# Merged products, another formula for |w|, an early one-column sine and a later modulation step in the generation of an S4 convolution kernel

## The chip, the core and the metric

The program runs on one core of one Trainium2 chip. Its metric is the device time of one execution in microseconds (us). A core has five engines with their own instruction streams: TensorE (PE in the profile, with weight loads as PEld), VectorE (DVE), ScalarE (ACT), GpSimd (POOL) and SyncE (SP). Here SyncE and GpSimd mainly issue DMAs. TensorE's clock is granted by a throttle; the profile gives it as a share of full speed.

## The reference

A block with 512 channels over 2048 positions: a layer norm with modulation, a long convolution per channel whose kernel K is built from a diagonal state space model, then a mixer and an MLP. The change lies in how K is built.

```python
dt = exp(log_dt)[:, None]
A, Bc, Cc = A_re + 1j*A_im, B_re + 1j*B_im, C_re + 1j*C_im
logdA, dB = dt * A, dt * Bc
P = exp(logdA[:, :, None] * l[None, None, :])        # l = 0 .. 2047
K = einsum("dn,dnl,dn->dl", Cc, P, dB).real          # 512 channels, 128 states
...
mod = (silu(c) @ w_mod).reshape(1, 6, 1, 512)
h = layernorm(x) * (1 + ca) + sa
x = x + ga * ssm_conv(h)                              # y = conv(h, K) + h * Dskip
...
```

With w = Cc * B, a channel's K[l] is the real part of a sum over 128 states of dt * w * exp(dt * A * l). Position l is split into a fine part (64 values) and a coarse one (32 values); the sum over states is then a matmul between a coarse factor, which carries w, and a fine one.

## The kernel before

The program has a preparation (lines 282 to 412), the generation loop (lines 531 to 564), and the transforms, the convolution, the mixer and the MLP behind it. All of it stands in an order written out by hand: each engine runs its instructions in the order of the program, and an instruction waits for the tiles that it needs.

*Preparation.* VectorE works on tiles of 128 x 512 (four groups of 128 channels on the partitions, 128 states each). It forms dt*A, w (`wr`, `wi`), the absolute values `ax`, `ay`, their larger `mc` and smaller `mn`, the ratio (with a first reciprocal, line 368), its arctangent `at0` on ScalarE, and out of it the phase of w in turns (`at`, lines 386 to 394). The weight |w| dt is `wn`: ScalarE takes the cosine of `at0`, VectorE its reciprocal (line 400), times `mc`, times dt. TensorE transposes `wn` (line 406) and ScalarE evicts it to `WN`. The phases are split into a high and a low part (`hilo`) and placed by matmuls with permutations (line 358, tiles `px`), evicted to `T1S`. In between, the modulation vectors are formed (`mod_parts`, `mod_sum`); lines 411 and 412 multiply two of them by a third.

*The loop.* A chunk k is 16 channels, 32 chunks in all; four chunks make a group t of 64 channels. For each chunk:

- `turns(k, cos)` forms the phase of both factors in turns with matmuls (lines 462 and 463, two halves of the array at a time; constants added and subtracted round them to the nearest turn), and ScalarE takes the sine or the cosine of the two 512 columns at once. It runs two chunks ahead.
- `exps(t, ...)` forms the magnitudes for a whole group on TensorE and ScalarE (five pieces), once in four chunks, in the chunk with k % 4 == 1. Sine and exponential need different tables of ScalarE, so the table is loaded twice per group (ACT_TABLE_LOAD).
- `weigh(t)` multiplies a part of the magnitudes by `WN` (line 261).
- `products(k)` on VectorE: `m1`, the coarse magnitude, as an outer product of two small factors (line 478); the fine factor `e0` with the sine in both signs (two instructions on line 482) and with the cosine (line 484); the coarse factor `e1` with the sine (483) and the cosine (485).
- `burst(k, ...)`: 64 small matmuls sum over the states (line 502); every second chunk ScalarE evicts the result to `KX`.
- `fill(n)`: n matmuls into a tile that is overwritten later (line 491), which keep TensorE busy.
- `side[k]`: the normalization of the input u (lines 423 to 430), its first transform (`u_dft`, evicted to `vs`, written to DRAM), and loads. `later` and `now` put evictions one chunk later.

Work tiles are rotated: `xx` (PSUM) has two buffers, the sine's and the cosine's tiles three, `e0` and `e1` two, `m1` one.

Of the kernel before, what the change touches and what calls it, by code (L numbers as in the profile page):

```python
# [109 lines left out]
def body(ctx, tc, A):  # L110
# [171 lines left out]
    with tc.manual_schedule():  # L282
# [59 lines left out]
        wr, wi, t0, t1 = tmp("wr"), tmp("wi"), tmp("t0"), tmp("t1")  # L342
        V.tensor_mul(wr, cr, br)
# [42 lines left out]
        V.tensor_scalar(at, at0, INV2PI, None, op0=OP.mult)  # L386
# [13 lines left out]
        V.reciprocal(wn, wn)  # L400
        V.tensor_mul(wn, wn, mc)
# [9 lines left out]
        V.tensor_mul(mods[1], mods[1], mods[2])  # L411
        V.tensor_mul(mods[0], mods[0], mods[2])
# [40 lines left out]
    def turns(k, cos):  # L453
        t, u = divmod(k, 4)
        r0 = slice(u // 2 * 64, u // 2 * 64 + 64)
        r1 = slice(64 - r0.start, 128 - r0.start)
        l0, l1, c = T0S[r0, t], T1S[r1, t * 2 + k % 2], slice(k % 2 * 512, k % 2 * 512 + 512)
        x = psx.tile([128, 1024], F32, name="xx")
        ops = [(l0, C0[r0, c], l1, C1[r1])] + [(ON[r0, i], MG[r0], ON[r1, i], MG[r1]) for i in (2, 0, 1)[1 - cos:]]
        ops.append((l0, C0N[r0, c], l1, C1N[r1]))  # L460
        for i, (la, ma, lb, mb) in enumerate(ops):
            T.matmul(x[:, :512], la, ma, start=(i == 0), stop=(i == len(ops) - 1))  # L462
            T.matmul(x[:, 512:], lb, mb, start=(i == 0), stop=(i == len(ops) - 1))  # L463
# [4 lines left out]
    trig = {}  # L468

    def products(k):  # L470
# [5 lines left out]
        f2 = lambda z: z.rearrange("p a b -> p (a b)")  # L476
        m1 = wk1.tile([128, 16, 32], F32, name="m1")
        V.tensor_mul(m1.rearrange("p d (x y) -> p d x y", x=4),
                     pt[:, :, None, :8].to_broadcast([128, 16, 4, 8]),
                     pt[:, :, 8:12, None].to_broadcast([128, 16, 4, 8]))  # L480
        for a in range(2):
            V.scalar_tensor_tensor(e0[:, 1, a], sn[:, 0], 1.0 - 2.0 * a, mg[:, a], op0=OP.mult, op1=OP.mult)  # L482
        V.tensor_mul(f2(e1[:, 1]), sn[:, 1], f2(m1))
        V.tensor_mul(e0[:, 0], cs[:, 0:1].to_broadcast([128, 2, 512]), mg)  # L484
        V.tensor_mul(f2(e1[:, 0]), cs[:, 1], f2(m1))  # L485
# [45 lines left out]
    with tc.manual_schedule():  # L531
        for k in range(2):
            trig[k] = turns(k, 0), turns(k, 1)
        weigh(0)
        for k in range(33):
            now, later = later, []
            if 1 in KP:
                fill(3)
            for f in now:
                f()  # L540
            if k + 2 < 32:
                trig[k + 2] = turns(k + 2, 0), turns(k + 2, 1)
            if k < 32:
# [622 lines left out]
```

## Time and profile before

| | |
|---|---|
| median of 3 runs | 769.93 us (769.35 to 771.09) |
| the profiled execution | 766.72 us, of it 764.9 us of span |
| mean granted TensorE clock | 0.952 |
| TensorE busy | 693.8 us (91%) |
| VectorE busy | 512.9 us (67%) |
| ScalarE busy | 332.8 us (44%) |
| GpSimd busy | 98.1 us (13%) |

The span is the time from the first to the last instruction. The shares are means over stages with different limits: in the preparation and the loop, the first 222 us, VectorE is nearly always busy, behind it TensorE alone. A row of the timeline reads: start, duration (both in us), engine, line, operation, written tile <- read tiles, sizes, count; in brackets the time the engine sat idle before it and what it waited for. A row that groups instructions ends with the busy time, the mean duration in ns and the idle time before. ACTIVATE instructions all carry line 118, that of a helper, and are told apart by their tiles: `sn` and `cs` are sine and cosine, `p` the magnitudes.

### The profile page before, as it was taken

To read this page: it belongs to the slowest core of one execution; us is meant where nothing else is said; L and a number is where in the kernel's file an instruction comes from. 1 tells how busy PE (TensorE), PEld (TensorE's weight loads), DVE (VectorE), ACT (ScalarE), POOL (GpSimd) and SP (SyncE) were. 2 spreads that over 40 slices of the span, in tenths; PEclk is the share of its full clock that TensorE was granted. 3 is DMA by queue.
4 is the path that set the end of the run, shared out by engine and by line. 5 is a ranking of instruction groups with operands and counts; after the bars stand their busy time and mean duration, and the time that the engine had idled before them with its cause. 6 is when DMAs were issued, how large, how long until landed. Compare 5 with 4: busy or idle time off the path is not lost. (4 is left out here: it accounts for less than half of the span.)

```text
span 764.9 us, 17371 instructions
## 1 busy us (share of the span) xinstructions
PE 693.8 (91%) x7340; PEld 540.2 (71%) x7340; DVE 512.9 (67%) x883; ACT 332.8 (44%) x540; POOL 98.1 (13%) x194
## 2 busy tenths in 40 slices
PE   2799999999989999995578799999999999999993
PEld 1356666665569656662368698999999998998992
DVE  8999999999873576774695696655565545353611
ACT  3678888887843445533133453312223121212120
POOL 1011121110000001000145110112021010100101
PEclk9999999999995899998789799999999999999997
DMA  9523282645259994884316701111110111101001
GB/s 299 164 66 83 71 235 77 168 131 149 57 130 258 243 334 152 274 251 167 137 40 230 246 29 28 29 38 46 32 52 15 42 29 28 28 28 28 9 20 27
DMA packets 51301, 85.51 MB, mean 112 GB/s; under 512 B 5300, under 2 KB 37944, under 8 KB 49560
## 3 DMA queue, kind: packets, MB, share of 16 engines
q1 hardware_dynamic: 44808, 57.92, 27.3%
q0 software_dynamic: 6416, 26.48, 10.5%
q8 instruction: 58, 0.95, 0.5%
q14 instruction: 19, 0.16, 0.1%
HBM read 58.17 MB, written 31.85 MB: 118 GB/s over the span
## 5 line engine op out<-in xcount | busy, mean ns | idle before, releaser
L118 ACT ACTIVATE gh<-pm 128x512 fp32r<-128x512 f32 (+1 forms) x48 | 26.9, 561 | 202.1 <-PE pm L784 202.1
L781 PE MATMUL pm<-nh,w3h 128*128 128x256 f32 (+1 forms) x352 | 87.9, 283 | 0.4 <-ACT nh L118 0.4
L782 PE MATMUL pm<-nh,w3l 128*128 128x256 f32 (+1 forms) x352 | 87.4, 281 | 0.0
L885 DVE TENSOR_TENSOR gl<-gf,gh 128x512 fp32r<-128x512 f32 (+1 forms) x48 | 30.9, 643 | 72.0 <-ACT gf L118 72.0
L894 PE MATMUL pa<-w4h,gh 128*128 128x512 f32 (+1 forms) x176 | 69.5, 395 | 0.0
L895 PE MATMUL pa<-w4l,gh 128*128 128x512 f32 (+1 forms) x176 | 68.9, 391 | 0.0
L781 PEld LDWEIGHTS pm<-nh,w3h 128*128 128x128 f32 (+1 forms) x352 | 65.4, 186 | 2.0 <-ACT nh L118 0.6
L782 PEld LDWEIGHTS pm<-nh,w3l 128*128 128x128 f32 (+1 forms) x352 | 65.6, 186 | 1.7
L784 PE MATMUL pm<-nl,w3h 128*128 128x256 f32 (+1 forms) x352 | 56.1, 282 | 0.0
L784 PEld LDWEIGHTS pm<-nl,w3h 128*128 128x128 f32 (+1 forms) x352 | 47.8, 186 | 0.1
L900 PE MATMUL pa<-w4h,gl 128*128 128x512 f32 (+1 forms) x176 | 47.8, 390 | 0.0
L462 PE MATMUL xx<-MG,ON 64*128 64x512 f32 x160 | 47.4, 391 | 0.0
L463 PE MATMUL xx<-MG,ON 64*128 64x512 f32 x160 | 47.4, 391 | 0.0
L482 DVE SCALAR_TENSOR_TENSOR e<-sn,p 128x512 f32<-128x512 f32 x64 | 41.2, 685 | 4.7 <-ACT sn L118 4.7
L841 DVE TENSOR_TENSOR h<-h,ph 128x512 f32<-128x512 f32 x16 | 11.0, 688 | 45.9 <-PE ph L840 45.9
L502 PEld LDWEIGHTS kp<-e,e 128*32 128x32 f32 x2048 | 30.1, 110 | 14.7 <-issue 9.7
L118 ACT ACTIVATE p<-xx 128x1024 f32<-128x1024 f32 (+1 forms) x40 | 38.2, 983 | 4.3 <-PE xx L254 3.1
L648 DVE TENSOR_TENSOR ma<-pk,us 128x512 f32<-128x512 f32 x32 | 21.9, 686 | 26.0 <-issue 18.2
L484 DVE TENSOR_TENSOR e<-cs,p 128x1024 f32<-128x1024 f32 x32 | 39.0, 1218 | 0.0
L118 ACT ACTIVATE z<-pz 128x512 f32<-128x512 f32 x32 | 17.4, 595 | 49.6 <-issue 33.9
L502 PE MATMUL kp<-e,e 128*32 128x64 f32 x2048 | 35.5, 221 | 2.8 <-DVE e L485 1.9
L900 PEld LDWEIGHTS pa<-w4h,gl 128*128 128x128 f32 (+1 forms) x176 | 33.0, 188 | 6.9
(223 smaller groups left out, 1862.5 us busy)
## 6 DMA issues: line engine op xcount, KB each, us to landing
VU<-vs SPq DMA_DIRECT2D x64, 128.0 KB, 2.6
ld<-VU SPq DMA_DIRECT2D x32, 256.0 KB, 8.2
ZT<-z POOLq DMA_DIRECT2D x16, 512.0 KB, 4.6
ld<-ZT SPq DMA_DIRECT2D x16, 512.0 KB, 5.6
Dw<-in_w POOLq DMA_DIRECT2D x8, 688.0 KB, 4.6
xu<-in_u SPq DMA_DIRECT2D x16, 256.0 KB, 6.7
KX<-in_u SPq DMA_DIRECT2D x16, 256.0 KB, 10.1
GD<-go POOLq DMA_DIRECT2D x16, 256.0 KB, 2.7
```

Source lines behind the costliest of these rows:

```text
L118: return S.activation(out, in_, f, bias=bias, scale=scale)
L462: T.matmul(x[:, :512], la, ma, start=(i == 0), stop=(i == len(ops) - 1))
L463: T.matmul(x[:, 512:], lb, mb, start=(i == 0), stop=(i == len(ops) - 1))
L482: V.scalar_tensor_tensor(e0[:, 1, a], sn[:, 0], 1.0 - 2.0 * a, mg[:, a], op0=OP.mult, op1=OP.mult)
L484: V.tensor_mul(e0[:, 0], cs[:, 0:1].to_broadcast([128, 2, 512]), mg)
L502: T.matmul(kp[32 * j:32 * j + 32, (k % 2) * 4 + g], e1[:, r, d], e0[:, r, :, d * 32:d * 32 + 32], start=(r == 0), stop=(r == 1), skip_grou ...
L781: T.matmul(p, wh[:, k, c], hi[k], start=(k == 0), stop=False)
L782: T.matmul(p, wl[:, k, c], hi[k], start=False, stop=False)
L784: T.matmul(p, wh[:, k, c], lo[k], start=False, stop=(k == 3))
L894: T.matmul(acc[i], gh[:m, e, s], W4h[:m, f], start=(f == 0), stop=False)
L895: T.matmul(acc[i], gh[:m, e, s], W4l[:m, f], start=False, stop=False)
L900: T.matmul(acc[i], gl[:m, e, s], W4h[:m, f], start=False, stop=(f == 10))
```

## The change

In the preparation, |w| becomes mc * cos(at0) + mn * sin(at0), with a second sine on ScalarE (`ws`) in the place of the reciprocal; the ratio goes to `mx` so that `mn` lives on; the scaling of the arctangent to turns moves from VectorE to ScalarE; `wn` and `ws` lie in columns of KX. The transposes of the weights and the third modulation vector move behind the first turns, and the two multiplications of modulation vectors to the end of chunk 1. In the loop, sine and cosine share one tile, so that the coarse factor is one product of 1024 columns; `m1` is formed for two chunks at once; the two sine products of the fine factor come first, and the first weighing behind them. A sine of a single column (`turn1`) follows the five magnitudes of a group. Of twelve fillers a group, five are left.

```diff
@@ preparation
+        wn, ws = KX[:, 7168:7680], KX[:, 7680:]
...
-        V.tensor_mul(mn, mn, mx)
-        at, at0, wn = tmp("at"), tmp("at0"), tmp("wn")
-        act(at0, mn, AF.Arctan)
+        V.tensor_mul(mx, mn, mx)
+        at, at0 = tmp("at"), tmp("at0")
+        act(at0, mx, AF.Arctan)
+        act(at, at0, scale=INV2PI)
         act(wn, at0, AF.Sin, scale=-1.0, bias=hpi)
+        act(ws, at0, AF.Sin)
...
-        V.tensor_scalar(at, at0, INV2PI, None, op0=OP.mult)
...
-        V.reciprocal(wn, wn)
         V.tensor_mul(wn, wn, mc)
+        V.tensor_mul(ws, ws, mn)
+        V.tensor_add(wn, wn, ws)
         V.tensor_tensor(as4(wn), as4(wn), by(dt), op=OP.mult)
-        wps = psu.tile([128, 512], F32, name="pu")
-        for i in range(4):
-            s = slice(i * 128, (i + 1) * 128)
-            T.transpose(wps[:, s], wn[:, s], ident)
-        act(WN, wps)
-        mod_parts(2)()
-        mod_sum(2)()
-        load_u(1)
-        V.tensor_mul(mods[1], mods[1], mods[2])
-        V.tensor_mul(mods[0], mods[0], mods[2])
@@ turns
-        o = wk.tile([128, 2, 512], F32, name="cs" if cos else "sn", bufs=3)
-        act(o.rearrange("p a b -> p (a b)"), x, AF.Sin, scale=-TWO_PI, bias=hpi if cos else 0.0)
-        return o
+        if not cos:
+            trig[k] = wk.tile([128, 2, 2, 512], F32, name="tr", bufs=3)
+        act(trig[k][:, 1 - cos].rearrange("p a b -> p (a b)"), x, AF.Sin, scale=-TWO_PI, bias=hpi if cos else 0.0)
...
+    turn1 = wk1.tile([128, 1], F32, name="turn1")
@@ products
-        sn, cs = trig.pop(k)
-        mg, pt = PE[t][0][u], PE[t][1][:, u]
+        tr = trig.pop(k)
+        mg = PE[t][0][u]
...
-        m1 = wk1.tile([128, 16, 32], F32, name="m1")
-        V.tensor_mul(m1.rearrange("p d (x y) -> p d x y", x=4),
-                     pt[:, :, None, :8].to_broadcast([128, 16, 4, 8]),
-                     pt[:, :, 8:12, None].to_broadcast([128, 16, 4, 8]))
         for a in range(2):
-            V.scalar_tensor_tensor(e0[:, 1, a], sn[:, 0], 1.0 - 2.0 * a, mg[:, a], op0=OP.mult, op1=OP.mult)
-        V.tensor_mul(f2(e1[:, 1]), sn[:, 1], f2(m1))
-        V.tensor_mul(e0[:, 0], cs[:, 0:1].to_broadcast([128, 2, 512]), mg)
-        V.tensor_mul(f2(e1[:, 0]), cs[:, 1], f2(m1))
+            V.scalar_tensor_tensor(e0[:, 1, a], tr[:, 1, 0], 1.0 - 2.0 * a, mg[:, a], op0=OP.mult, op1=OP.mult)
+        if k == 0:
+            weigh(0)
+        if u % 2 == 0:
+            m1 = m1s[0] = wk1.tile([128, 2, 512], F32, name="m1")
+            pt = PE[t][1][:, u:u + 2].rearrange("p a d c -> p (a d) c")
+            V.tensor_mul(m1.rearrange("p a (d x y) -> p (a d) x y", x=4, y=8),
+                         pt[:, :, None, :8].to_broadcast([128, 32, 4, 8]),
+                         pt[:, :, 8:12, None].to_broadcast([128, 32, 4, 8]))
+        V.tensor_mul(e0[:, 0], tr[:, 0, 0:1].to_broadcast([128, 2, 512]), mg)
+        V.tensor_mul(e1.rearrange("p r d q -> p r (d q)"), tr[:, :, 1], m1s[0][:, u % 2:u % 2 + 1].to_broadcast([128, 2, 512]))
         return e0, e1
@@ the loop
-        for k in range(2):
-            trig[k] = turns(k, 0), turns(k, 1)
-        weigh(0)
+        turns(0, 0)
+        turns(0, 1)
+        wps = psu.tile([128, 512], F32, name="pu")
+        for i in range(4):
+            T.transpose(wps[:, i * 128:i * 128 + 128], wn[:, i * 128:i * 128 + 128], ident)
+        act(WN, wps)
+        late = mod_parts(2)
+        turns(1, 0)
+        late()
+        late = mod_sum(2)
+        turns(1, 1)
+        late()
+        load_u(1)
         for k in range(33):
             now, later = later, []
-            if 1 in KP:
-                fill(3)
...
             if k + 2 < 32:
-                trig[k + 2] = turns(k + 2, 0), turns(k + 2, 1)
+                turns(k + 2, 0)
+                turns(k + 2, 1)
...
                     fill(3)
                     for u in range(2, 5):
                         exps(k // 4 + 1, u, u + 1)
-                        fill(2)
+                        if u < 4:
+                            fill(1)
+                    act(turn1, hpi, AF.Sin)
...
+            if k == 1:
+                V.tensor_mul(mods[1], mods[1], mods[2])
+                V.tensor_mul(mods[0], mods[0], mods[2])
             for f in side[k]:
                 f()
```

More of the change, by code (lines that the diff above doesn't have):

```diff
@@ L463, in turns @@
             T.matmul(x[:, 512:], lb, mb, start=(i == 0), stop=(i == len(ops) - 1))
-        o = wk.tile([128, 2, 512], F32, name="cs" if cos else "sn", bufs=3)
-        act(o.rearrange("p a b -> p (a b)"), x, AF.Sin, scale=-TWO_PI, bias=hpi if cos else 0.0)
-        return o
+        if not cos:
+            trig[k] = wk.tile([128, 2, 2, 512], F32, name="tr", bufs=3)
+        act(trig[k][:, 1 - cos].rearrange("p a b -> p (a b)"), x, AF.Sin, scale=-TWO_PI, bias=hpi if cos else 0.0)
     trig = {}
+    turn1 = wk1.tile([128, 1], F32, name="turn1")
+    m1s = {}
     def products(k):
         t, u = divmod(k, 4)
-        sn, cs = trig.pop(k)
-        mg, pt = PE[t][0][u], PE[t][1][:, u]
+        tr = trig.pop(k)
+        mg = PE[t][0][u]
         e0 = wk.tile([128, 2, 2, 512], F32, name="e0")
         e1 = wk.tile([128, 2, 16, 32], F32, name="e1")
-        f2 = lambda z: z.rearrange("p a b -> p (a b)")
-        m1 = wk1.tile([128, 16, 32], F32, name="m1")
-        V.tensor_mul(m1.rearrange("p d (x y) -> p d x y", x=4),
-                     pt[:, :, None, :8].to_broadcast([128, 16, 4, 8]),
-                     pt[:, :, 8:12, None].to_broadcast([128, 16, 4, 8]))
-        for a in range(2):
[L482 to L485, printed above, removed]
+        for a in range(2):
+            V.scalar_tensor_tensor(e0[:, 1, a], tr[:, 1, 0], 1.0 - 2.0 * a, mg[:, a], op0=OP.mult, op1=OP.mult)
[9 more added lines that the diff above has]
+        V.tensor_mul(e1.rearrange("p r d q -> p r (d q)"), tr[:, :, 1], m1s[0][:, u % 2:u % 2 + 1].to_broadcast([128, 2, 512]))
         return e0, e1
```

## The prediction

> **What bounds the kernel now.** I read the page first, then the busy times by stretch, one stretch for each of the eight groups of 64 channels of the generation loop (cut where the weighing on line 261 runs, so a stretch holds four chunks), then VectorE's instructions in order of time, then ScalarE's and TensorE's around a change of group.
>
> ```profile
> 86.60:108.30 21.70, 20.93 (x313) 13.27 (x317) 21.37 (x35) 17.97 (x21) 3.38 (x5) 1.00 0.64 180
> ...
> 177.60:200.90 23.30, 21.85 (x368) 13.82 (x371) 21.62 (x34) 18.78 (x22) 3.04 (x5) 1.00 0.52 145
> 200.90:222.50 21.60, 19.75 (x429) 12.54 (x421) 18.78 (x27) 15.55 (x21) 0.00 (x0) 1.00 0.27 57
> sum 180.50, PE 173.36 PEld 108.80 DVE 172.04 ACT 147.50 POOL 26.02; mean PE 21.67 PEld 13.60 DVE 21.50 ACT 18.44 POOL 3.25
> ```
>
> A row has the stretch and its length, then the busy time (and count) of TensorE, its weight loads, VectorE, ScalarE and GpSimd, and TensorE's granted clock. The loop is 180.5 of the 764.9 us of the span. VectorE is busy 172.0 of it and TensorE 173.4, so two engines share the bound, with ScalarE at 147.5 behind. But part of TensorE's time is filler: 84 matmuls of line 491 whose result nobody reads. In a group where VectorE has enough other work the stretch is VectorE's sum (21.37 of 21.70); later groups last 23.3 for much the same 21.6.
>
> One chunk of VectorE's work in the steady state, and the first and the last of eight places where two chunks follow each other directly:
>
> ```profile
> 87.76 0.66 DVE L478 TENSOR_TENSOR m<-p 128x512 f32<-128x512 f32 x1
> 88.33 1.29 DVE L482 SCALAR_TENSOR_TENSOR e<-sn,p 128x512 f32<-128x512 f32 x2
> 89.54 0.69 DVE L483 TENSOR_TENSOR e<-sn,m 128x512 f32<-128x512 f32 x1
> 90.14 1.22 DVE L484 TENSOR_TENSOR e<-cs,p 128x1024 f32<-128x1024 f32 x1
> 91.28 0.69 DVE L485 TENSOR_TENSOR e<-cs,m 128x512 f32<-128x512 f32 x1
> 91.88 0.75 DVE L429 SCALAR_TENSOR_TENSOR xu<-xu,lum,modu 128x512 f32<-128x512 f32 x1
> ...
> 103.42 0.68 DVE L485 TENSOR_TENSOR e<-cs,m 128x512 f32<-128x512 f32 x1
> 104.14 0.69 DVE L478 TENSOR_TENSOR m<-p 128x512 f32<-128x512 f32 x1
> ...
> 217.51 0.69 DVE L485 TENSOR_TENSOR e<-cs,m 128x512 f32<-128x512 f32 x1
> 218.23 0.69 DVE L478 TENSOR_TENSOR m<-p 128x512 f32<-128x512 f32 x1
> ```
>
> What counts is the distance from start to start, not the duration: instructions overlap by about 0.08 us. Line 478 costs 0.57, the two of line 482 1.21, 483 0.60, 484 1.14, 485 0.60, together 4.12. Where 478 comes straight behind 485 the distance is 0.72 and not 0.60, because it overwrites the one m1 tile that 485 is reading in those eight places.
>
> Now a change of group, the last one (ScalarE, then VectorE), and the waits of the whole loop:
>
> ```profile
> 192.10 1.03 ACT L118 ACTIVATE sn<-xx 128x1024 f32<-128x1024 f32 x1
> ...
> 194.38 1.28 ACT L118 ACT_TABLE_LOAD   x1
> ...
> 200.80 0.59 ACT L118 ACTIVATE KX<-kp 128x512 f32<-128x512 f32 x1
> 201.64 1.09 ACT L118 ACTIVATE vs<-pu 128x512 f32<-128x512 f32 x2 [0.25 <-ACT KX L118]
> 203.67 1.28 ACT L118 ACT_TABLE_LOAD   x1 [0.94 <-PE xx L463]
> 204.97 1.02 ACT L118 ACTIVATE sn<-xx 128x1024 f32<-128x1024 f32 x1
> ...
> 202.81 0.68 DVE L478 TENSOR_TENSOR m<-p 128x512 f32<-128x512 f32 x1
> 206.02 1.29 DVE L482 SCALAR_TENSOR_TENSOR e<-sn,p 128x512 f32<-128x512 f32 x2 [2.53 <-ACT sn L118]
> ...
> DVE e L482 <- ACT sn L118: 4.7, 4, 2.5
> DVE p L261 <- ACT p L118: 0.9, 1, 0.9
> ```
>
> ScalarE needs its exponentials' table for the five magnitudes and the sine's table after them. The second load waits 0.94 for TensorE's turns (their fillers and the u transform come first), then loads for 1.28, and only then comes the sine that VectorE waits for. In all VectorE waits 4.7 + 0.9 = 5.6 us inside the loop, always at such a change.
>
> The stage before the loop is one VectorE chain:
>
> ```profile
> 27.81 0.42 DVE L386 TENSOR_SCALAR tp_at<-tp_at 128x512 f32<-128x512 f32 x1
> ...
> 35.08 3.35 DVE L400 RECIPROCAL tp_wn<-tp_wn 128x512 f32<-128x512 f32 x1
> 38.45 0.69 DVE L401 TENSOR_TENSOR tp_wn<-tp_wn,tp_mc 128x512 f32<-128x512 f32 x1
> ...
> 39.79 0.68 DVE L411 TENSOR_TENSOR modu<-modu 128x512 f32<-128x512 f32 x1
> 41.69 0.43 DVE L261 TENSOR_TENSOR p<-p,WN 128x256 f32<-128x256 f32 x1 [1.22 <-ACT WN L118]
> ```
>
> **The change part by part.** *Reciprocal and table arithmetic.* The reciprocal (3.37 to the next start) goes; a multiply and an add come, at the 0.60 of line 483 and, for the one that waits for the one before it, the 0.72 of line 485 above, so -2.0. Line 386 becomes a ScalarE copy (-0.42). The weights, now ready where line 411 starts, are so at 39.8 - 2.4 = 37.4. ScalarE gets this copy and a second sine, about 0.6 each like the 128x512 KX eviction above; they push four evictions for the modulation back by 1.2, for which no VectorE instruction waits before line 411's place.
>
> *Products first, weights later.* The first chunk's sine products no longer wait for the weights, but for the phases:
>
> ```profile
> 35.21 3.05 PE L358 MATMUL xx<-hilo,PB 128*128 128x512 f32 x7 [0.23 <-DVE hilo L317]
> 38.19 0.79 PE L462 MATMUL xx<-C,T0S 64*128 64x512 f32 x1
> 32.00:34.00 2.00, 0.00 (x0) 0.00 (x0) 1.70 (x3) 0.21 (x2) 0.00 (x0) 1.00 0.82 283
> 34.00:36.00 2.00, 1.28 (x4) 0.84 (x5) 1.53 (x2) 0.43 (x1) 0.00 (x0) 0.90 1.16 391
> 36.00:38.00 2.00, 2.00 (x6) 1.25 (x4) 2.00 (x1) 1.03 (x1) 0.00 (x0) 0.50 1.02 221
> 38.00:40.00 2.00, 2.00 (x13) 1.56 (x13) 1.93 (x4) 1.02 (x1) 0.00 (x0) 0.75 0.62 127
> 38.30 1.02 ACT L118 ACTIVATE T1S<-xx 128x1024 fp32r<-128x1024 f32 x1 [0.68 <-PE xx L358]
> ```
>
> The turns start at 38.19 - 0.42 = 37.8; four pairs of matmuls take 1.6 (0.79, then 0.26 a pair, as the fillers below show at full clock); the sine of 1.0 then ends at 40.4, and the products begin there instead of the weighing at 41.69: 1.3 earlier. New waits: the weighing is now behind the cosine on ScalarE (40.6 to 41.7) and the weights' eviction, so VectorE idles some 0.65 at 41.6, with m1 and all other products of the first chunk queued behind. Line 411 loses the hole at 40.5 that hid it and costs 0.61. So the start gains nearly nothing, unless TensorE's clock stays up. It granted 0.50 after the hole that the row 32 to 34 shows: 0.4 us of the next row's 2, all of the third and half of the fourth, some 3.4 us from 35.6 on. In the new order the modulation's matmuls come 1.2 later and shrink that hole to some 1.5 us. At full clock the seven matmuls of line 358 and the first turns take half, 1.5 us less on the path. The rows cannot say; I give it 0.6, that is 0.9 us.
>
> [...]
>
> The modulation's last part (8 matmuls, two evictions, four loads of u) moves behind the first turns; those loads are wanted by the fifth statistics, in chunk 6, over 20 us later, so I cost them at nothing. Without that cover those statistics would wait for the loads to land.
>
> *Merged products.* 483 and 485 become one 128x1024 multiply of 484's form: 0.60 + 0.60 - 1.14 = 0.06 in each of 32 chunks, 2 us. Two m1 become one of 1024: 2 x 0.57 to 0.60 against 1.14, 0.8 us in 16 pairs; the m1 pattern at 1024 is not in the trace, and between 1.14 and two single ones lies no more than that. The 0.12 behind 485 goes eight times, 1.0, as other products now stand in between. Together 3.8.
>
> [...]
>
> *Fillers and the early table.* 49 of the 84 fillers go:
>
> ```profile
> L491 PE MATMUL kp<-CE,TES 128*128 128x512 f32 x84 | 27.7, 430 | 0.0
> 104.63 1.32 PE L491 MATMUL kp<-CE,TES 128*128 128x512 f32 x5
> ```
>
> Five in a row take 1.32, so 0.26 each: seven fewer are 1.8 us of TensorE's time at each of seven changes of group. TensorE falls from the 21.67 of the mean to 19.9 a group, well below VectorE's 21.5. The one-column sine puts the table load right behind the magnitudes, where ScalarE would wait for the turns. Its own cost is not in the trace; it lies between nothing and the 0.59 of a 128x512 eviction, on an engine with 3 us to spare a group (18.4 against 21.5). I take 0.2.
>
> At the last change, in the old frame: the magnitudes end at 200.9, the load at 202.2, the one-column sine at 202.4, the KX eviction at 203.0, the vs at 204.1 and the sine at 205.1, where it ended at 206.0: 0.9 sooner, and ScalarE is now what it waits for. VectorE wants it 0.6 sooner than before, as m1 no longer stands in front. But the turns that fed 192.10 come sooner too: the 1.8 us of fillers of the group before had made TensorE late in using up the products, and with it in everything behind them. So of 2.53 there stay 2.53 + 0.6 - 0.9 - 1.8 = 0.4, and half a microsecond by which VectorE comes sooner after a shorter group. The other waits (0.9, and 4.7 - 2.5 = 2.2 over three changes) fall below zero by the same sum. I keep 1.0 of the 5.6; the bounds are 0 and 5.6.
>
> **Sum**, against the profiled execution (span 764.9, 766.7 with what lies around it): start 1.3 - 0.65 - 0.61, nearly 0; clock 0.9; products 3.8; waits 5.6 - 1.0 = 4.6. Together 9.3 us, 757.4 in its frame. The runs shown have a median 3.2 above it, 769.93: 760.6. Everything behind the loop waits for its last chunk and moves along.
>
> **The rivals.** *The waits stay* (ScalarE, not TensorE, ends the wait at each change): the first sine stays 2.5 late, as at 206.02. Then 9.3 - 4.6 = 4.7, about 765. For it speaks that ScalarE is nearly without a pause from 194.38 to 202.7; against it, that three changes out of seven had no wait.
>
> *One tile for sine and cosine*: if the products of the sine now wait for both, each of seven changes pays the cosine's 1.1 us: 9.3 - 7.7 = 1.6, 768.3. Against it: line 462 started at 38.19, before the eviction at 38.30 had written the second half of the phase tile (T1S), so the order goes by parts of a tile.
>
> *Slower: the clock falls in the loop.* The fillers keep TensorE busy while it waits for ScalarE's magnitudes. If fewer of them let the clock drop, each drop costs 1.7 us (3.4 us at 0.50, as behind 35.6). One a change is absorbed (19.9 + 1.7 = 21.6); from the second on TensorE needs 23.3 a group against 22.7 now: some 4 us more than before, 774. Against it: five fillers and 3 us of magnitudes' matmuls still lie in that stretch.
>
> [...]
>
> *More than forecast*: the first stage behind the loop,
>
> ```profile
> L590 PE MATMUL py<-FK,KX 32*128 32x64 f32 x16 | 2.0, 273 | 0.0
> ...
> L590 PE MATMUL py<-FK,KX 32*128 32x64 f32 x113 | 24.6, 415 | 0.0
> ```
>
> is at half clock in all but its first 16 of 128 rounds (a matmul takes 415 ns against 273, and a round 24.6/113 = 0.22 against 2.0/16 = 0.12). If the drop comes one 3.4 us stretch later, 28 rounds more run at 0.12, 2.8 us off; if it comes at once, 1.6 us on. With no wait left at the changes (1.0 more) and a late drop: 756.8, and with the start's full 1.5 another 0.6 off. So 755 to 757.
>
> **How the numbers follow.** Forecast (757 to 763.5) 0.50; waits stay (763.5 to 767) 0.24; one tile 0.06; slower 0.11; more 0.09. The range 755.5 to 768.5 holds all but the slower case and the tails. A difference under 0.2%, 1.5 us, can't be told from none here: faster 0.84, same 0.05, slower 0.11.
>
> **What would show it.** Right: VectorE's last product near 213 instead of 222.5; no reciprocal but the first; the sine's load directly behind the fifth magnitude; starts 1.14 apart for the merged product; line 491 35 times; granted clock 1.00 throughout the loop. Wrong: first sine products waiting 2 us at the changes, a granted clock of 0.5 inside the loop, a merged product much over 1.22 us, or a stretch behind the loop longer than the 542 us it has now.

## The result and the profile after

| | before | after |
|---|---|---|
| median (4 runs each, side by side) | 770.51 us (769.35 to 772.17) | 759.25 us (757.67 to 762.26) |
| the profiled execution | 766.72 us, of it 764.9 us of span | 759.28 us, of it 757.5 us of span |
| VectorE's last product ends (start + duration) | 222.46 us | 210.61 us |
| fillers (lines 491 and 489) | 84 | 35 |
| mean granted TensorE clock | 0.952 | 0.946 |

The ratio after/before is 0.9857 [0.9821, 0.9893]: 1.4% faster. The forecast was 760.6.

First VectorE in order of time, from the timeline of the changed kernel: the first chunk, one chunk of the steady state, and the end of the loop.

```profile
39.21 1.29 DVE L473 SCALAR_TENSOR_TENSOR e<-tr,p 128x512 f32<-128x512 f32 x2 [1.85 <-ACT tr L118]
40.85 0.43 DVE L261 TENSOR_TENSOR p<-p,WN 128x256 f32<-128x256 f32 x1 [0.35 <-ACT WN L118]
...
203.65 1.22 DVE L479 TENSOR_TENSOR m<-p 128x1024 f32<-128x1024 f32 x1
204.78 1.22 DVE L482 TENSOR_TENSOR e<-tr,p 128x1024 f32<-128x1024 f32 x1
205.92 1.22 DVE L483 TENSOR_TENSOR e<-tr,m 128x1024 f32<-128x1024 f32 x1
207.05 1.28 DVE L473 SCALAR_TENSOR_TENSOR e<-tr,p 128x512 f32<-128x512 f32 x2
...
209.39 1.22 DVE L483 TENSOR_TENSOR e<-tr,m 128x1024 f32<-128x1024 f32 x1
213.23 0.42 DVE L573 TENSOR_TENSOR KX<-DS,KX 128x128 f32<-128x128 f32 x1 [2.62 <-ACT KX L118]
```

The merged product starts 1.13 before its successor (205.92 to 207.05), and so does the doubled `m1` (203.65 to 204.78). The last product ends at 210.61, 11.85 us earlier than before. The addition on line 573 is the first VectorE work behind the loop; it stood at 224.31.

The groups of instructions of the changed kernel (busy time, mean ns | idle time before them):

```profile
L473 DVE SCALAR_TENSOR_TENSOR e<-tr,p 128x512 f32<-128x512 f32 x64 | 41.1, 683 | 1.8 <-ACT tr L118 1.8
...
L483 DVE TENSOR_TENSOR e<-tr,m 128x1024 f32<-128x1024 f32 x32 | 39.0, 1218 | 0.0
```

The 1.8 us that sine products wait are those of the very first (1.85 at 39.21). At the changes of group nothing is left of the 4.7 + 0.9 us of before. ScalarE at a change of group, from its timeline:

```profile
56.54 2.82 ACT L118 ACTIVATE p<-xx 128x1024 f32<-128x1024 f32 x3 [0.16 <-PE xx L254]
59.38 1.28 ACT L118 ACT_TABLE_LOAD   x1
60.67 0.20 ACT L118 ACTIVATE turn<-hpi 128x1 f32<-128x1 f32 x1
60.78 0.58 ACT L118 ACTIVATE KX<-kp 128x512 f32<-128x512 f32 x1
61.26 1.02 ACT L118 ACTIVATE tr<-xx 128x1024 f32<-128x1024 f32 x1
```

The load stands directly behind the magnitudes. The sine of one column lasts the 0.20 that was taken for it, and the next instruction starts 0.11 behind its start. The loop by stretches (length, then busy time and count of TensorE, its weight loads, VectorE, ScalarE, GpSimd, then granted clock, DMA share, GB/s), four of the eight groups and the sum of all:

```profile
84.14:105.33 21.19, 20.37 (x367) 12.70 (x363) 20.89 (x28) 18.80 (x23) 3.42 (x5) 1.00 0.68 195
...
127.33:150.06 22.73, 22.25 (x391) 13.46 (x379) 22.32 (x30) 20.68 (x26) 3.43 (x5) 1.00 0.68 180
...
171.24:192.44 21.20, 20.29 (x331) 12.43 (x320) 20.90 (x29) 18.69 (x24) 3.42 (x5) 1.00 0.57 159
192.44:211.00 18.56, 16.54 (x420) 10.69 (x420) 18.05 (x22) 13.64 (x18) 0.00 (x0) 0.99 0.36 75
sum 170.00, PE 160.43 PEld 100.13 DVE 167.19 ACT 145.13 POOL 26.64; mean PE 20.05 PEld 12.52 DVE 20.90 ACT 18.14 POOL 3.33
```

Where two late groups took 23.3 us before for 21.4 and 21.6 of VectorE's work, each full group now lasts what VectorE's work in it lasts, and 0.3 to 0.4 more: 20.9 of 21.2 in most, 22.3 of 22.7 in the longest. VectorE waits for nothing there and sets the pace; TensorE is idle between 0.5 and 1.1 us in a full group behind the first, so it is not far behind.

Not all of the 11.85 us reached the end of this execution: its span is only 7.4 us shorter. TensorE and VectorE behind the loop, from the timeline and then the stretches:

```profile
210.66 1.89 PE L500 MATMUL kp<-e,e 128*32 128x64 f32 x64 [2.02 <-DVE e L483]
...
249.88 0.69 DVE L660 TENSOR_TENSOR ma<-pk,us 128x512 f32<-128x512 f32 x1 [5.15 <-PE pk L649]
```

```profile
210.00:212.00 2.00, 1.34 (x53) 1.34 (x57) 0.61 (x1) 0.00 (x0) 0.00 (x0) 0.69 0.97 198
...
248.00:250.00 2.00, 2.00 (x62) 1.76 (x58) 0.12 (x1) 0.36 (x2) 0.00 (x0) 0.92 0.57 162
```

The clock fell just after the start of the last burst, ahead of which TensorE had paused for 2.02 us (0.69 of full speed on average between 210 and 212: 0.94 between 210.5 and 210.8, 0.50 from there on), and the 64 matmuls of that burst took 1.89 us. Before, they took 1.10 behind a pause of 1.87, and the clock held at 1.00 to 226:

```profile
222.52 1.10 PE L502 MATMUL kp<-e,e 128*32 128x64 f32 x64 [1.87 <-DVE e L485]
...
256.82 0.69 DVE L648 TENSOR_TENSOR ma<-pk,us 128x512 f32<-128x512 f32 x1 [4.08 <-PE pk L637]
```

So the first multiply of the convolution came only 6.94 us earlier (249.88 against 256.82). Whether that is a price of the change is taken up below.

### The profile page after: what moved, and what is told of

The parts are those of the page before. It is cut to its first block, busy times and chain, and to the rows that moved or that the text cites. A ratio compares the mean times of both kernels' runs of the same rounds, so it can differ in the third digit from the quotient of the medians.

```text
span 757.5 us, 17206 instructions
## 1 busy us (share of the span) xinstructions
PE 682.1 (90%) x7291; PEld 532.4 (70%) x7291; DVE 506.4 (67%) x835; ACT 333.2 (44%) x549; POOL 98.3 (13%) x194
## 4 chain that ended last, share of the span: by engine, by line
PE 43%; DVE 4%; ACT 1%; POOL 1%; DMA 1%; issue 1%; POOLq 0%; DVEq 0%; ACTq 0%
PE pm L793 7%; PE pm L794 7%; PE pm L796 7%; PE pa L907 5%; PE pa L906 5%; PE pa L912 5%; PE ph L852 2%; PE ph L850 2%; PE ph L849 2%; PE pT L755 2%; DVE h L738 1%; DMA GD<-go 1%; DVE st L733 1%; DVE h L737 1%; DVE nl L763 0%
## 5 line engine op out<-in xcount | busy, mean ns | idle before, releaser
L473 DVE SCALAR_TENSOR_TENSOR e<-tr,p 128x512 f32<-128x512 f32 x64 | 41.1, 683 | 1.8 <-ACT tr L118 1.8
L482 DVE TENSOR_TENSOR e<-tr,p 128x1024 f32<-128x1024 f32 x32 | 39.0, 1218 | 0.0
L483 DVE TENSOR_TENSOR e<-tr,m 128x1024 f32<-128x1024 f32 x32 | 39.0, 1218 | 0.0
```

The lines of the kernel that those rows point to most:

```text
L473: V.scalar_tensor_tensor(e0[:, 1, a], tr[:, 1, 0], 1.0 - 2.0 * a, mg[:, a], op0=OP.mult, op1=OP.mult)
L482: V.tensor_mul(e0[:, 0], tr[:, 0, 0:1].to_broadcast([128, 2, 512]), mg)
```

## The experiments

The theory was that TensorE set the pace, through its fillers, and that the cut fillers bring the gain, to which the rest of the change can then add; its rival, that VectorE's own work (products, reciprocal, order at the start) brings it. Where an experiment asks something narrower, its expectation sets out its own theories. Each kernel ran beside runs of the kernel before on its chip. "Last product ends" is the end of VectorE's last product in the profiled execution, worked out as start + duration. The "loop end" of the expectations is another mark, the start of the addition into KX behind it (224.31 before, 213.23 after). The waits are those inside the loop, of VectorE for sine, cosine, magnitudes or the burst. "Clock" is that of the stretch 42 to 205.

| kernel | fillers a group | median, us | ratio to before | last product ends | waits | clock |
|---|---|---|---|---|---|---|
| before | 12 | | 1 | 222.46 | 5.6 | 1.00 |
| after | 5 | 759.25 | 0.9857 [0.9821, 0.9893] | 210.61 | 0 | 1.00 |
| b1_sched | 5 | 763.03 | 0.9915 [0.9885, 0.9945] | 216.37 | 0 | 0.98 |
| b2_merge | 12 | 768.59 | 0.9990 [0.9976, 1.0003] | 221.81 | 8.4 | 1.00 |
| b3_prep | 12 | 768.54 | 1.0002 [0.9983, 1.0021] | 222.70 | 3.4 | 1.00 |
| b4_hole | 12 | 768.79 | 1.0001 [0.9982, 1.0019] | 222.66 | 5.8 | 1.00 |
| a3_fill12 | 12 | 769.16 | 0.9991 [0.9970, 1.0012] | 221.53 | 8.2 | 1.00 |
| a2_no_turn | 5 | 758.90 | 0.9855 [0.9824, 0.9885] | 211.86 | 1.2 | 0.99 |
| a1_recip | 5 | 757.38 | 0.9844 [0.9809, 0.9879] | 211.35 | 0.2 | 0.99 |
| d1_fill3 | 3 | 761.15 | 0.9901 [0.9867, 0.9935] | 212.97 | 2.2 | 0.97 |
| d2_fill11 | 2 | 772.97 | 1.0045 [1.0018, 1.0071] | 223.14 | 12.2 | 0.88 |
| a4_no_fill | 0 | 773.30 | 1.0039 [1.0013, 1.0065] | 229.36 | 18.1 | 0.87 |

### The old kernel with fewer fillers and the early table alone

```diff
@@ the kernel before: the loop
-            if 1 in KP:
-                fill(3)
...
                         exps(k // 4 + 1, u, u + 1)
-                        fill(2)
+                        if u < 4:
+                            fill(1)
+                    act(turn1, hpi, AF.Sin)
```

> The kernel before with only the fillers cut (12 to 5 a group) and the one-column sine added. Theory A: VectorE's waits in the loop (5.6 us) go, its instructions stay; loop end 224.3 - 5.6 = 218.7, or up to 219.7 where m1 in front of the sine product still hides nothing. Theory B (the later groups, 23.3 long for 21.6 of VectorE's work, lose more than the listed waits): 217 or less.

The waits at the changes are gone with nothing else changed (line 483 is here the sine product); the rows are of the groups, then of the timeline:

```profile
L483 DVE SCALAR_TENSOR_TENSOR e<-sn,p 128x512 f32<-128x512 f32 x64 | 41.1, 683 | 0.0
```

```profile
41.74 0.42 DVE L261 TENSOR_TENSOR p<-p,WN 128x256 f32<-128x256 f32 x1 [1.24 <-ACT WN L118]
...
86.64 0.41 DVE L261 TENSOR_TENSOR p<-p,WN 128x256 f32<-128x256 f32 x1
108.31 0.41 DVE L261 TENSOR_TENSOR p<-p,WN 128x256 f32<-128x256 f32 x1
...
153.99 0.42 DVE L261 TENSOR_TENSOR p<-p,WN 128x256 f32<-128x256 f32 x1
175.68 0.41 DVE L261 TENSOR_TENSOR p<-p,WN 128x256 f32<-128x256 f32 x1
197.47 0.41 DVE L261 TENSOR_TENSOR p<-p,WN 128x256 f32<-128x256 f32 x1
...
215.69 0.68 DVE L486 TENSOR_TENSOR e<-cs,m 128x512 f32<-128x512 f32 x1
```

Groups of 21.7 and 21.8 us (153.99 to 175.68 to 197.47) stand where before had 23.3 twice. The last product ends 6.1 us earlier: all of the 5.6 of waits, and half a microsecond more. The addition starts at 219.01, in the range of theory A.

### The whole change with the old fillers

```diff
@@ the kernel after: the loop
             now, later = later, []
+            if 1 in KP:
+                fill(3)
...
                         exps(k // 4 + 1, u, u + 1)
-                        if u < 4:
-                            fill(1)
+                        fill(2)
```

> The changed kernel with all twelve fillers a group, the one-column sine kept. Theory A (TensorE is the bound with the fillers): 7 x 1.8 us of work come back to TensorE, which then needs 20.05 + 1.8 = 21.9 a group against VectorE's 20.9; loop end later by 4 to 8, 217 to 221, with VectorE waiting at the changes of group. Theory B (the early table load alone is enough): 213 to 214.5.

Nearly nothing is left of the gain. The addition starts at 223.38, theory A and past its upper end of 221. First a row of the groups, then the stretch from 42 to 205:

```profile
L473 DVE SCALAR_TENSOR_TENSOR e<-tr,p 128x512 f32<-128x512 f32 x64 | 41.2, 684 | 11.5 <-ACT tr L118 11.3
```

```profile
42.00:205.00 163.00, 157.69 (x2536) 98.99 (x2528) 151.90 (x200) 137.09 (x161) 25.55 (x40) 1.00 0.45 119
```

VectorE has less to do (151.90 us of the stretch) and waits 8.2 us inside the loop (the 11.5 less the wait for the first sine), while TensorE is busy 157.69 of 163: what VectorE saves, it spends waiting for turns. In this execution the clock had also fallen in the preparation (0.72 between 30 and 42), so that the first product came at 40.83 and not at 39.21; the loop's end is not corrected for that.

### The merged products alone

```diff
@@ the kernel before: products
-        sn, cs = trig.pop(k)
+        tr = trig.pop(k)
...
-        V.tensor_mul(f2(e1[:, 1]), sn[:, 1], f2(m1))
...
-        V.tensor_mul(f2(e1[:, 0]), cs[:, 1], f2(m1))
+        V.tensor_mul(e1.rearrange("p r d q -> p r (d q)"), tr[:, :, 1], m1s[0][:, u % 2:u % 2 + 1].to_broadcast([128, 2, 512]))
```

(`m1` for two chunks and the joint tile `tr` too, as in the change; the sine products stay behind `m1`, and the twelve fillers stay.)

> The kernel before with only the products merged (one coarse product of 1024 columns, m1 for two chunks, one tile for sine and cosine), m1 still ahead of the sine products, twelve fillers, no one-column sine. Theory A (distances from start to start, 3.8 us in all, but TensorE sets the pace of the later groups): VectorE's work falls by 3.8, its waits rise, loop end 221 to 223.5. [...] A wait of the sine products for the cosine would show as over 1 us more at each change of group.

```profile
L485 DVE SCALAR_TENSOR_TENSOR e<-tr,p 128x512 f32<-128x512 f32 x64 | 41.1, 684 | 7.5 <-ACT tr L118 7.3
```

In this row of its groups the waits for the sine have grown from 4.7 to 7.3 us, and the last product comes 0.65 earlier. The joint tile costs nothing: at the longest of these waits the sine has been written at 205.49, the product starts at 205.53, and the cosine is only done at 206.50. Without the cut fillers merging gains next to nothing (addition at 223.66, about the upper end of theory A).

### The preparation alone

```diff
@@ the kernel before: preparation and first chunk
+        act(at, at0, scale=INV2PI)
         act(wn, at0, AF.Sin, scale=-1.0, bias=hpi)
+        act(ws, at0, AF.Sin)
...
-        V.reciprocal(wn, wn)
         V.tensor_mul(wn, wn, mc)
+        V.tensor_mul(ws, ws, mn)
+        V.tensor_add(wn, wn, ws)
...
+        if k == 0:
+            weigh(0)
```

(and the transposes, the modulation and `load_u(1)` moved as in the change; in every chunk `m1` stands behind the sine products.)

> The kernel before with only the preparation changed (|w| without reciprocal, first products ahead of the weights, third modulation vector later, order of the loop's products as changed but not merged), twelve fillers, no one-column sine. Theory A: the first product starts at 39.2 as in the changed kernel, the clock stays up there, and 1.3 to 2.5 us stay at the loop's end: 221.8 to 223, if the later waits for the sine do not eat them. Theory B (TensorE sets the pace of the loop): the gain of the start is eaten, 224.

The first product starts at 40.35 and not at 42.76, and the last ends at 222.70, 0.24 later than before. The head start of 2.4 us is gone by the end of the loop, and the addition starts at 224.56: theory B. Theory A's 39.2 for the first product was missed, since the clock did not stay up (0.86 between 30 and 42).

### TensorE's clock in the preparation

```diff
@@ the kernel before: preparation
         load_u(0)
+        hole = psu.tile([128, 512], F32, name="pu")
+        for _ in range(12):
+            T.matmul(hole, TES[:, 0], CE[:, :512], start=True, stop=True, skip_group_check=True)
```

> The kernel before with twelve extra matmuls (128x512, result not used) on TensorE in the hole before the phases' second part, at 31.4 to 34.5. Theory A (the hole dropped the clock to 0.50 behind 35.6): the granted clock stays 1.00 from 30 to 42, the seven matmuls of line 358 (359 here or shifted) take 1.9 instead of 3.05 as in the changed kernel, and the first cosine and sine come 1 to 1.5 us earlier. Theory B (the clock fell for another reason): it falls again between 35 and 39 and nothing moves.

With twelve more fillers in TensorE's pause the granted clock between 30 and 42 us was 1.00 and not 0.86, and the seven matmuls took 1.88: theory A for the clock. The first sine started only 0.3 earlier, though (41.24, 41.56 before), and the first cosine later (44.63, 42.95 before). The first weighing came at 41.37 instead of 41.69, since in this order it waits for the weights and not for the turns. The last product ends at 222.66: nothing is left of it either.

### The reciprocal put back

```diff
@@ the kernel after: preparation
-            act(ws, at0, AF.Sin)
...
+            V.reciprocal(wn, wn)
             V.tensor_mul(wn, wn, mc)
-            V.tensor_mul(ws, ws, mn)
-            V.tensor_add(wn, wn, ws)
```

> The changed kernel with the reciprocal back in the place of the second sine, the multiply and the add (the order of the loop kept). Measured by the start of the addition into KX that ends the loop (224.31 before, 213.23 changed). Theory A (the first products wait for the phases, the weights have slack behind them): the weights are ready 2.0 us later, at 39.4, just where TensorE comes to their transposes; the weighing moves from 40.85 by at most 0.6 and the loop ends at 213.2 to 213.9. Theory B (the reciprocal was on the path): the whole 2.0 us come back, loop end 215.2.

The first weighing stood at 40.91 against 40.85 and the addition at 213.20: theory A. The interval of the time lies over that of the change: the new formula for |w| is worth nothing that these runs can tell. Once the first sine products go ahead of the weighing, the weights have the time that the phases take.

### The one-column sine taken out

```diff
@@ the kernel after: the loop
                             fill(1)
-                    act(turn1, hpi, AF.Sin)
```

> The changed kernel without the one-column sine, five fillers a group as changed. Theory A (fillers and the late table load each caused the waits, TensorE being late through the fillers; with the fillers gone there is slack): waits for the sine of 0 to 1.5 us in all, loop end 213.2 to 214.8. Theory B (the early table load removes the waits): the waits for the sine come back, 4 to 5 us in all, loop end 217 to 218.

One wait of 1.2 us for a cosine appears, and the last product ends 1.25 later. But this wait is not at a change of group. Rows of this run (TensorE, VectorE, and the clock of a stretch), then of the change, then of d1_fill3, which has the one-column sine:

```profile
43.52 1.89 PE L225 MATMUL pu<-xu,sp 128*128 128x512 f32 x2 [1.66 <-ACT xu L118]
48.78 1.22 DVE L481 TENSOR_TENSOR e<-tr,p 128x1024 f32<-128x1024 f32 x1 [1.19 <-ACT tr L118]
44.00:46.00 2.00, 2.00 (x6) 0.57 (x6) 1.97 (x4) 0.00 (x0) 0.22 (x2) 0.50 0.00 0
```

```profile
43.53 1.12 PE L225 MATMUL pu<-xu,sp 128*128 128x512 f32 x2 [1.66 <-ACT xu L118]
```

```profile
48.78 1.23 DVE L482 TENSOR_TENSOR e<-tr,p 128x1024 f32<-128x1024 f32 x1 [1.20 <-ACT tr L118]
```

The wait is in the second chunk, ahead of the first table load of the loop (54.73). The clock had fallen to 0.50 behind a pause of 1.66 us on TensorE; in the change it held behind the same pause (1.00 between 44 and 46), and in d1_fill3 it fell too (0.66 between 42 and 47) and left the same wait. From the second weighing to the last the run takes 129.51 us (64.22 to 193.73) and the change 129.49 (62.95 to 192.44): at the changes of group the one-column sine gains nothing that can be seen once the fillers are cut, and all of the 1.25 is the clock's. The addition at 213.72 is in the range of theory A; in the medians no difference is seen.

### No fillers, two, three

```diff
@@ the kernel after: the loop (a4_no_fill; d1_fill3 drops only the fill(1), d2_fill11 only the fill(3))
-                    fill(3)
                     for u in range(2, 5):
                         exps(k // 4 + 1, u, u + 1)
-                        if u < 4:
-                            fill(1)
```

> The changed kernel without any filler. Rival of the clock: TensorE's granted clock falls below 1.00 inside the loop at the changes of group, each drop costs 1.7 us of TensorE's work, and the loop ends at 215 or later. My theory: TensorE's holes stay under 2 us, the clock stays at 1.00, and since VectorE sets the pace the loop ends within 0.5 of 213.2.

> The changed kernel with three fillers a group (those behind the burst), without the two between the magnitudes. Theory A (the clock needs dense matmuls among the magnitudes' quarter-array ones, whatever TensorE's busy share): the granted clock falls below 1.00 in some of the seven changes of group, loop end 215 to 225. Theory B (three are enough): clock 1.00, loop end 213 to 214.

> The changed kernel with two fillers a group (those between the magnitudes), without the three behind the burst. Theory A: as few dense matmuls as that let the clock fall at most changes of group, loop end 218 to 230, near the 231.2 of none. Theory B (their place among the magnitudes is what counts): clock 1.00, loop end 213 to 214.

Without any, the kernel is slower than before, and the addition starts at 231.21: the rival of the clock came, and my theory failed. The stretches of a4_no_fill, then TensorE's timeline at one change of group:

```profile
42.00:205.00 163.00, 150.42 (x2358) 92.22 (x2356) 149.00 (x196) 130.82 (x152) 25.22 (x40) 0.87 0.44 117
...
128.00:133.00 5.00, 4.03 (x73) 2.54 (x74) 4.97 (x8) 4.99 (x5) 1.96 (x3) 0.91 0.00 0
```

```profile
128.62 1.10 PE L500 MATMUL kp<-e,e 128*32 128x64 f32 x64
...
130.30 0.73 PE L254 MATMUL xx<-CE,TES 32*128 32x512 f32 x2 [0.58 <-ACT p L118]
131.21 0.73 PE L254 MATMUL xx<-CE,TES 32*128 32x512 f32 x2 [0.19 <-ACT p L118]
132.14 1.01 PE L249 MATMUL xx<-CE,TES 128*128 128x512 f32 x2 [0.20 <-ACT p L118]
```

The clock was 1.00 between 127 and 132 and 0.66 between 132 and 137; if it went from 1.00 straight to 0.50, a mean of 0.91 over the stretch from 128 puts the fall at about 132.1 (0.9 us at 0.50), an estimate. From 128.62 up to there TensorE had paused three times, for 0.58, 0.19 and 0.20 us, and worked otherwise, on matmuls that each fill 32 of the array's columns (line 500, 128*32 in the rows) or 32 of its rows (line 254, 32*128).

Three fillers behind the burst nearly hold the clock: it falls at two of seven changes (0.79 in the lowest 5 us of each) and once ahead of them (0.66), 0.97 in the mean, and the last product comes 2.4 us later than with five. More than half of that comes from the fall in the second chunk, ahead of any filler: the second weighing is 1.3 late already (64.21 against 62.95). The addition at 214.82 lies between the two theories. Two among the magnitudes do not hold it: 0.88, and the addition at 225.00, theory A. Of the six profiled kernels with five, the clock held at every change of group in the changed kernel, a2_no_turn, c3_dense and d4_dense_half; in b1_sched it dipped at two (0.98 in the mean) and in a1_recip at one (0.99). That is 3 of 42 changes of group.

### The first stage behind the loop

The first stage's matmuls in the profile of the change, a row of its groups:

```profile
L602 PE MATMUL py<-FK,KX 32*128 32x64 f32 x128 | 28.1, 417 | 0.0
```

At 417 ns all 128 rounds are at half clock (0.50 granted from 212 to 243). To see whether it can be lifted, one dense matmul was set ahead of each of its eight passes, 512 columns (c3_dense) or 256 (d4_dense_half); what it writes is overwritten.

```diff
@@ the kernel after: first stage behind the loop
         kv = KX.rearrange("p (g x) -> p g x", g=64)
+        T.matmul(ps[0].rearrange("p a b -> p (a b)"), ident, KX[:, :512], start=True, stop=True, skip_group_check=True)
         for gl in range(8):
```

> The changed kernel with one dense fp32 matmul (128x128 by 128x512, result overwritten) ahead of each of the eight rounds of the first stage behind the loop, where the clock stands at 0.50 although TensorE is busy throughout. Theory A (the stage's own matmuls, 32 rows by 64 columns, count for too little, and one dense one of about 1.1 us in three lifts it): granted clock 1.00 in most of the stage, its 27 to 28 us become about 23, and the end comes 2 to 5 us earlier. Theory B (not enough): clock 0.50, and eight of them cost 2.2 each, 15 to 18 us more.

> As the run with dense matmuls in the first stage behind the loop, with 256 columns in the place of 512. Theory A: the clock is held with half of them too, the stage takes about 19 us and the end comes 5 to 9 us earlier. Theory B: it falls, and they cost about 1.1 each, 8 to 9 us more.

The medians are 776.33 (ratio 1.0092 [1.0066, 1.0119]) and 768.09 (0.9976 [0.9947, 1.0005]). Theory B came in both: the clock stayed down in both profiles (0.50 from 218 to 258 in c3_dense, from 213 to 253 in d4_dense_half). A stretch of the stage and the added matmuls in c3_dense, from the stretches and the groups:

```profile
219.00:224.00 5.00, 5.00 (x62) 3.38 (x62) 1.29 (x2) 1.08 (x2) 0.00 (x0) 0.50 1.05 250
```

```profile
L599 PE MATMUL pk<-KX,ident 128*128 128x512 f32 x16 | 16.3, 1124 | 1.2 <-DVE KX L573 1.2
```

From the addition behind the loop to the first multiply, 50.8 us pass (213.63 to 264.46) against 36.7 in the change (213.23 to 249.88): 14.2 more, most of the 16.3 us that the added matmuls take; in d4_dense_half it is 8.4 more (213.70 to 258.72). One of ten executions of d4_dense_half took 759.62 us, the others 766.23 to 770.84. Its mean granted clock was 0.959, that of the others 0.938 to 0.945, so the clock was up for longer in it; where, and whether in this stage, stays open, since it has no profile.

c3_dense is a control for the start, too: up to the loop's end it is the changed kernel, but its clock fell in the preparation (0.86 between 30 and 42). Its timeline:

```profile
40.39 1.29 DVE L473 SCALAR_TENSOR_TENSOR e<-tr,p 128x512 f32<-128x512 f32 x2 [1.84 <-ACT tr L118]
...
210.56 1.22 DVE L483 TENSOR_TENSOR e<-tr,m 128x1024 f32<-128x1024 f32 x1
...
213.63 0.42 DVE L573 TENSOR_TENSOR KX<-DS,KX 128x128 f32<-128x128 f32 x1 [1.85 <-ACT KX L118]
```

It starts 1.18 us later than the change and ends its products 1.17 later (211.78): with VectorE as the only bound, what is lost at the start stays lost to the end of the loop. d4_dense_half, whose clock fell there too, says the same: 1.25 at the start, 1.24 at the end.

## Why the prediction was right, point by point

The likeliest case came: 9.3 us were forecast, and the medians lie 11.3 apart. The 2 us beyond the forecast lie in the sizes of the terms. The chain of the argument held: TensorE, late through its fillers, makes ScalarE's sine late, and with the fillers cut VectorE's own sum is the pace.

**The sum, term by term**, in VectorE's frame (11.85 us to the end of the last product):

- *Waits, 4.6 forecast, 6.1 measured* (b1_sched). I had kept 1.0 of the 5.6 for a VectorE that comes sooner; none came back, since TensorE was far enough ahead, and 0.5 more went that no row names.
- *Clock in the preparation, 0.9 forecast, 1.2 measured* (after against c3_dense). The seven matmuls that took 3.05 took 1.89, and the stretches show no fall (the row that had 0.50 before):

```profile
34.76 1.89 PE L359 MATMUL xx<-hilo,PB 128*128 128x512 f32 x7 [0.23 <-DVE hilo L317]
```

```profile
36.00:38.00 2.00, 1.81 (x13) 1.10 (x13) 1.33 (x2) 1.71 (x2) 0.00 (x0) 1.00 1.15 302
```

  But it was luck as much as the smaller pause. Of ten profiled kernels with this preparation (one of them with the reciprocal), the clock was 1.00 between 30 and 42 us in five and between 0.58 and 0.86 in the other five. My 0.6 was about right as a chance; the change does not secure it. The hole that I looked at did shrink, from 3.11 us to 1.46. What I did not look at is the pause ahead of the modulation's matmuls (line 225), which the change widens from 1.66. The change, then c3_dense, where the clock fell at 30.1:

```profile
30.58 1.98 PE L225 MATMUL pu<-xu,sp 128*128 128x512 f32 x4 [2.51 <-ACT xu L118]
```

```profile
30.61 3.41 PE L225 MATMUL pu<-xu,sp 128*128 128x512 f32 x4 [2.76 <-ACT xu L118]
```

  In the five profiles whose clock stayed up this pause is 1.99 to 2.51 us, in the other five 2.69 to 3.03; in four of these the clock fell between 29.7 and 31.7, in the fifth (d4_dense_half) at 35.5. Why the pause varies, and whether it is the cause, no run settles.
- *Products 3.8 and the rest of the start nearly 0 forecast, 4.6 measured together* (b1_sched to after is 5.76, less 1.17 of the clock). Seven groups, from one weighing to the next up to 192.44 in the change and 197.47 in b1_sched, are shorter by 4.14 in all, of which the first alone gives 0.99 (part of its work now lies ahead of its weighing) and each of the third to sixth 0.47 to 0.51 (the third: 21.67 in the rows of b1_sched, 21.19 in the change). Eight times 0.48 is the 3.8; the 0.8 that is left is spread over the others and I have not taken it apart.

**What the sum hides is that its terms hang on one another.** Each was priced as if it stood alone. With twelve fillers the merged products gave 0.65 us and the preparation -0.24, and both with the early table 0.93 (222.46 to 221.53). With five fillers the products and the preparation gave 5.76 (b1_sched to after). The clock in the preparation has a part in this difference: it was up in the change and down in b3_prep (0.86) and a3_fill12 (0.72), whose first products came 1.1 and 1.6 us later. Two engines shared the bound; a saving on VectorE counts only after TensorE has been relieved. All five profiles with twelve fillers end the loop within 1.2 us of each other, though VectorE's busy time between 42 and 205 is anything from 151.9 to 156.7. The prediction named the shared bound in its first paragraph and put TensorE below VectorE without the seven fillers, but did not say that its other terms count only then: its sum is right because the filler cut is part of it.

**The reciprocal.** Priced at -2.0, with the path going to the phases instead: a1_recip shows that nothing depends on it, which the prediction's start term implied and did not say.

**The early table load.** The forecast did not part it from the fillers and took 0.9 us of the last change's wait off for it. In the changed kernel it is worth nothing that can be seen at the changes (129.51 us without it, 129.49 with it), and with twelve fillers it does not end the waits either (8.2 us in a3_fill12). So the 6.1 of both go to the fillers, although the old kernel with five fillers and without it was not run.

**The rivals.** *The waits stay*: ScalarE does not end the wait once TensorE is ahead; b1_sched shows none. *One tile*: in b2_merge, with the joint tile, the sine products start before the cosine is done. *The clock falls in the loop*: with five it did not in the change; with none it does, at all seven changes (0.50 to 0.66 in the lowest 5 us of each), and the medians of a4_no_fill and a2_no_turn, run side by side, lie 14.4 apart. What I set against it, five fillers and 3 us of matmuls in that stretch, did not say how few fillers would do, and in the expectation of a4_no_fill I went by the length of TensorE's holes, under 2 us. That was the wrong test: the clock fell at pauses of 0.58, 0.19 and 0.20 us, the only ones between 128.62 and the fall at about 132.1, among matmuls that each fill 32 columns or 32 rows of the array. That the part of the array is the cause is not shown: in the first stage behind the loop four such matmuls, one for each 32 rows, start within 0.02 us of one another, and the clock is down there too (0.50). What makes it fall no run settles. The chance of 0.11 was not too small for five fillers, but nothing that I gave told five from three or two (0.97 and 0.88 in the mean).

**Behind the loop.** I said "moves along" and named more than 542 us there as a sign of being wrong; it is 546.9 in the profile of the change (757.5 less 210.61) against 542.4 before. That looks like a matter of the single execution: the work there is the same in ten of the experiments' kernels, all but c3_dense and d4_dense_half, and in their profiles it takes from 542.6 us (a1_recip, with the new loop: 753.9 of span less 211.35) to 547.3 (b2_merge, with the old fillers: 769.1 less 221.81). The span of a1_recip is 11.0 shorter than that of before. The prediction had this as part of "more than forecast", with 1.6 us on for an early fall; 4.1 stood in this profile (11.08 at the addition, 6.94 at the first multiply), since the clock also came back later, some 4.5 us behind the stage's last matmul (243.8, and back at 248.3 by the 0.92 of its row) and not some 2 (251.8 and 254.0):

```profile
254.00:256.00 2.00, 2.00 (x56) 1.54 (x56) 0.00 (x0) 1.61 (x6) 0.00 (x0) 0.99 1.09 262
```

The profiled execution of before took 766.72 us, less than all four beside the change (769.35 to 772.17), and that of after was at its median (759.28 against 759.25). That is why the spans differ by 7.4 and the medians by 11.3.

No version beat the changed kernel beyond its interval; the medians of a1_recip and a2_no_turn are lower, but the intervals lie over each other.

## What to carry to other kernels

Where two engines are both near full in a loop, price an edit against the one that ends the waits, and try the edits alone and together: those on the other engine look worthless until the first has been made. Fillers that hold the clock are a dose: here twelve made TensorE the bound, five held the clock at 39 of 42 changes and left VectorE without waits in the changed kernel, three let it fall in places, and two or none lost more than the fillers had cost. A gain or a loss that rests on where the clock falls must be seen in several executions before it is counted, and a wait in one profile should be put beside the clock of that moment before an edit is blamed for it.

## What the runs showed of the hardware that was not expected

- The granted clock falls while TensorE works: 0.50 in the first stage behind the loop with TensorE busy 5.00 of 5 us, in matmuls on 32 rows each. One of its stretches in the changed kernel:

```profile
216.00:221.00 5.00, 5.00 (x100) 5.00 (x100) 1.42 (x3) 1.26 (x3) 0.00 (x0) 0.50 1.05 270
```

- One dense 128x512 matmul in each of eight passes (two instructions of 1.12 us) does not lift it there (0.50 between 219 and 224 in c3_dense), though in the loop five fillers of 128x512 (0.26 us each) in a group of 21 us are the difference between 1.00 and 0.87 (after against a4_no_fill).
- Behind the same pause of 1.66 us on TensorE, ending at 43.5, the clock fell in a2_no_turn (0.50 between 44 and 46) and d1_fill3 (0.66 between 42 and 47) and held in the change (1.00 between 44 and 46).
- The same instructions of the preparation ran at clocks from 0.58 to 1.00 in ten kernels that differ only later (or, in one, in the weights), for up to 2.9 us at the first product (39.21 in the change, 42.10 in a4_no_fill).
